# Linear attention and an MLP on one core: chunk one's state from products of 128 rows, alternating output columns, half loads without the zero lanes, and four loads under way

## The chip, the cores and the metric

The kernel runs on one core of a Trainium2 chip as one launch. The metric is the device time of a launch in microseconds (us); the kernel before took 490.62 us, the median of three runs (490.49 to 491.47).

## What is computed

```python
for t in range(S):                                   # S = 768, r, k, v: (4, 8, 768, 48) fp32
    cur = np.einsum('bhd,bhe->bhde', u[None] * kt, vt)
    y[:, :, t] = np.einsum('bhd,bhde->bhe', rt, state + cur)
    state = w[None, :, :, None] * state + np.einsum('bhd,bhe->bhde', kt, vt)
x = y.transpose(0, 2, 1, 3).reshape(3072, 384)
h = x @ w_in                                         # 384 -> 2048
out = (0.5 * h * (1 + erf(h / sqrt(2)))) @ w_out     # 2048 -> 384
```

w and u have one value for each head and channel. All of it is fp32.

## The kernel before, in words

**Attention.** The 768 positions are cut into 6 chunks of 128 positions, in halves h of 64. The 8 heads are taken as 4 pairs, in the order `PAIRS` = 3, 0, 1, 2. A group (`gi`, 0 to 23) is one pair in one chunk, for all 4 batches; groups 0 to 3 are chunk one, and I call them g0 to g3. A group loads two tiles: T (in_rkT) holds r and k transposed, head 0 of the pair on lanes 0 to 47 and head 1 on lanes 64 to 111, with zeros on lanes 48 to 63 that are read along; N (in_rkv) holds k and v by rows of positions.

The steps of a group of chunk one (`first_group`) are these. `prepare` multiplies T by a table E of powers of w (DVE, L426), N's k by the decay WN (POOL, L433), and makes KB = k * u * w (ACT, L444). `scores` (PE, L465) forms k.r into the banks A, `own` the same with KB, `gains` (PE, L476) the sum of k v over 64 positions for each half, which the states are made from, and two `select`s (DVE, L551) put the scores into Am. `gaps` (PE, L515) spreads pair 3's result x3 into the unused lanes of Y for the other three pairs; `old` (PE, L484) adds state times r, `new` (PE, L502) Am times v. `keep` takes Y out of PSUM: an ACT cast into the high part (L565) and a DVE subtraction for the low part (L566). The state after half one is an ACT copy (L532, Sb), the state after half two a DVE multiply and add on two lane quarters (L521, Sa). WN is made from a table of powers by four transposes (PE, L354) and an ACT copy (L357). The table itself is built on DVE: five doublings (L327, 112x8 up to 112x8x15), the power w^32, its reciprocal (L339) and three multiplications of 256 elements.

**MLP.** The weights come in 16 loads of 768 KB into three buffers (raw). Each is split into a high part wh and a low part wl: on ACT wb (L382), wa (L379), the second pass wb (L385) and wh (L391), on DVE wa (L387, L389) and wl (L393). For each chunk there are 16 MLP steps j, 96 in all: nine matmuls of 512 columns for the first layer (L649; high by high, then wl, then the low x), the gelu on ACT (L679), the high and low part of its result on DVE (L680, L681), and nine matmuls of the second layer (L692). During chunk one's 16 steps the PE also does the groups of chunk two, and each step needs a weight that has just been split.

**What sets the order.** A planner written into the kernel (class `Plan`) gives each step a cost and a due time and writes the engines' instruction streams in that order. Where it sees PE idle it puts in "heats" (L311), matmuls on zeros that nobody reads. The loads follow a list, `LOADS` (t0, t1, n0, t2, n1, ...); by `in_turn` a load is issued when the load two places ahead of it in the queue has landed (the first three go at once). T0 and T1 are loaded with 112 lanes, `BARE` = 2; from T2 on a load is two halves of 48 lanes, and the zero lanes are set once by a memset (POOL, L294).

Of the kernel before, what the change touches and what calls it, by code (L numbers as in the profile page):

```python
# [150 lines left out]
def rwkv_gelu_mlp(tc, rkT, rkv, wuT, uN, wmlp, r, k, vT, w, u, out):  # L151
    nc = tc.nc
    with ExitStack() as ctx:
# [31 lines left out]
        E = sb([LP, 2, NP, 2, HALF], F32, "E")  # L185
        P32 = sb([LP, 2, 2 * NP], F32, "P32")
# [139 lines left out]

        def powers():
            nc.vector.memset(one(E0, MID), 1.0)  # L330
            nc.vector.tensor_scalar(out=one(E0, MID + 1), in0=w_sb.unsqueeze(2), scalar1=WMIN, scalar2=WMAX,
                                    op0=ALU.max, op1=ALU.min)
            n = 1
            while n < MID:
                m = min(n, MID - 1 - n)
                times_one(E0[:, :, MID + n + 1:MID + n + 1 + m], E0[:, :, MID + 1:MID + 1 + m], one(E0, MID + n))
                n *= 2
            times_one(P32[:, 0].unsqueeze(2), one(E0, MID + 16), one(E0, MID + 16))
# [609 lines left out]
```

## Time and profile before

| what | us |
|---|---|
| median of three runs | 490.62 |
| the profiled execution | 491.24 |
| its span in the profile | 489.4 |
| PE busy in the span | 477.2 |
| DVE busy | 275.0 |
| ACT busy | 175.8 |
| POOL busy | 67.1 |

The profiled execution took 1.84 us more than its span, for what lies around it, and 0.62 us more than the median. The granted clock was 0.996 of full speed as a mean over the span. PE means TensorE's matmuls, PEld the loading of their stationary operand, which goes beside them. A row of the timeline has the start, the duration, the engine, the line, the operation, the tile written from the tiles read, the count, and in brackets how long the engine had been idle and what ended that.

### The profile page before, as it was taken

Reading aid. Unit: us, or ns where it says so; the run is one execution under the profiler, and the core shown is the slowest. Engines: PE = TensorE matmul, PEld = TensorE weight load, DVE = VectorE, ACT = ScalarE, POOL = GpSimd, SP = SyncE. Lnnn points to the kernel's source line nnn. Section 1 sums busy time; section 2 is a strip of 40 time slices with the busy share of each in tenths; the row PEclk is TensorE's granted clock in tenths of the full one; section 3 lists DMA queues with packets and bytes.
Section 4 is the critical chain, followed back from the end, with each engine's and each line's share of the span. In section 5 each row is a group of like instructions: output and inputs, shape, how many; then the busy total and the mean of one; then the engine's idle time right before and its main releaser. Section 6 shows DMA issues by size and latency. Waiting matters only on the chain.

```text
span 489.4 us, 11700 instructions
## 1 busy us (share of the span) xinstructions
PE 477.2 (98%) x5096; PEld 387.2 (79%) x5096; DVE 275.0 (56%) x446; ACT 175.8 (36%) x353; POOL 67.1 (14%) x85
## 2 busy tenths in 40 slices
PE   7899999999999999999999999999999999999995
PEld 5777787888888887788888878888888887888884
DVE  7689989896646556526536646544654522322221
ACT  6487989843133133131332321331331311211111
POOL 4202101102302022202022022021121100000000
PEclk9999999999999999999999999999999999999998
DMA  6867686513212313303203403123403000100002
GB/s 173 251 205 228 201 252 197 165 37 121 83 34 61 92 37 89 115 10 84 61 33 92 147 1 92 38 57 92 131 17 92 1 11 12 67 1 1 0 0 70
DMA packets 13192, 42.24 MB, mean 86 GB/s; under 512 B 2160, under 2 KB 2544, under 8 KB 13136
## 3 DMA queue, kind: packets, MB, share of 16 engines
q1 hardware_dynamic: 13136, 41.43, 28.9%
q8 instruction: 42, 0.69, 0.6%
q14 instruction: 14, 0.11, 0.1%
HBM read 34.74 MB, written 4.72 MB: 81 GB/s over the span
## 4 chain that ended last, share of the span: by engine, by line
PE 93%; DVE 4%; DMA 1%; issue 1%; SPq 0%; DVEq 0%
PE Hp L649 41%; PE O L692 40%; PE A L465 3%; PE Y L484 3%; PE Y L502 2%; PE Y L476 1%; PE AE L311 1%; PE Y L692 1%; DMA T<-in_rkT_dram 1%; DVE wa L389 1%; DVE Am L551 1%; DVE T L426 0%; PE A L311 0%; DVE wl L393 0%; PE Y L515 0%
## 5 line engine op out<-in xcount | busy, mean ns | idle before, releaser
L649 PE MATMUL Hp<-xx,wh 128*128 128x512 f32 x576 | 166.5, 396 | 0.6 <-ACT wh L391 0.4
L680 DVE CAST gh<-gf 128x512 fp32r<-128x512 f32 x95 | 47.4, 499 | 167.8 <-ACT gf L679 166.8
L679 ACT ACTIVATE gf<-Hp 128x512 f32<-128x512 f32 x96 | 57.4, 597 | 232.9 <-PE Hp L649 219.6
L649 PEld LDWEIGHTS Hp<-xx,wh 128*128 128x128 f32 x576 | 106.9, 188 | 25.9 <-ACT wh L391 1.1
L649 PE MATMUL Hp<-xx,wl 128*128 128x512 f32 x288 | 83.5, 397 | 1.3 <-DVE wl L393 1.1
L692 PE MATMUL O<-gh,wh 128*128 128x512 f32 (+1 forms) x285 | 82.3, 396 | 0.0
L692 PE MATMUL O<-gl,wh 128*128 128x512 f32 (+1 forms) x285 | 80.6, 390 | 0.0
L692 PE MATMUL O<-gh,wl 128*128 128x512 f32 (+1 forms) x285 | 80.6, 390 | 0.0
L681 DVE TENSOR_TENSOR gl<-gf,gh 128x512 fp32r<-128x512 f32 x95 | 74.1, 780 | 10.3 <-DVE gh L680 0.5
L649 PEld LDWEIGHTS Hp<-xx,wl 128*128 128x128 f32 x288 | 53.8, 188 | 15.1 <-DVE wl L393 2.4
L692 PEld LDWEIGHTS O<-gh,wh 128*128 128x128 f32 x285 | 52.2, 188 | 12.5 <-issue 0.3
L692 PEld LDWEIGHTS O<-gl,wh 128*128 128x128 f32 x285 | 52.6, 188 | 11.7
L692 PEld LDWEIGHTS O<-gh,wl 128*128 128x128 f32 x285 | 52.5, 188 | 11.6
L456 ACT ACTIVATE Am<-diag,cs 128x64 f32<-128x64 f32 x120 | 31.7, 338 | 30.4 <-DVE cs L451 30.4
L430 POOL TENSOR_TENSOR Nb<-Nb 128x384 f32<-128x384 f32 x15 | 15.6, 1037 | 125.5 <-DMA Nb<-in_rkv_dram 110.5
L433 POOL TENSOR_TENSOR Nb<-Nb,WN 128x384 f32<-128x384 f32 x20 | 23.5, 1175 | 52.1 <-DMA Nb<-in_rkv_dram 23.0
L426 DVE TENSOR_TENSOR Tb<-Tb,E 112x1024 f32<-112x1024 f32 x20 | 25.2, 1258 | 2.8 <-DMA Tb<-in_rkT_dram 2.7
L521 DVE SCALAR_TENSOR_TENSOR Sb<-Sa,E,Y 48x192 f32<-48x192 f32 x40 | 16.5, 413 | 10.8 <-ACT xx L565 7.0
L493 POOL MEMSET turn<- 1x1 f32 x19 | 1.7, 89 | 130.1 <-PE Y L484 130.1
L448 POOL TENSOR_TENSOR Nb<-Nb,u_sb 128x384 f32<-128x384 f32 x15 | 18.6, 1239 | 0.1
L551 DVE COPY_PREDICATED Am<-past,A 128x512 f32<-128x512 uint32 x24 | 17.7, 738 | 0.4
L565 ACT CAST xx<-Y 112x512 fp32r<-112x512 f32 (+1 forms) x18 | 10.6, 587 | 20.3 <-PE Y L476 14.3
(107 smaller groups left out, 402.0 us busy)
## 6 DMA issues: line engine op xcount, KB each, us to landing
raw<-in_wmlp_dram SPq DMA_DIRECT2D x16, 768.0 KB, 5.2
Nb<-in_rkv_dram SPq DMA_DIRECT2D x15, 576.0 KB, 4.0
Tb<-in_rkT_dram SPq DMA_DIRECT2D x40, 192.0 KB, 3.5
out_dram<-raw SPq DMA_DIRECT2D x5, 768.0 KB, 3.7
Nb<-in_rkv_dram SPq DMA_DIRECT2D x5, 384.0 KB, 3.8
xx<-x SPq DMA_DIRECT2D x30, 64.0 KB, 2.3
N<-in_rkv_dram SPq DMA_DIRECT2D x4, 384.0 KB, 4.0
T<-in_rkT_dram SPq DMA_DIRECT2D x2, 448.0 KB, 4.9
```

The lines of the kernel that those rows point to most:

```text
L426: add("dve", sdve(1024), LATER if g.gi else -10 ** 5, lambda: nc.vector.tensor_tensor(out=flat, in0=flat, in1=E[:, 0, g.p].rearrange("l h ...
L430: add("pool", pool(DM), LATER, lambda: nc.gpsimd.tensor_tensor(out=g.n[:, 0], in0=g.n[:, 0], in1=g.n[:, 1], op=ALU.mult), r=[g.K], w=[g.R])
L433: it = nc.gpsimd.tensor_tensor(out=g.kn, in0=g.kn, in1=WN[:, g.p].rearrange("s j d -> s (j d)").unsqueeze(1).to_broadcast([C, NB, 2 * D]), ...
L448: add("pool", pool(DM), LATER, lambda: nc.gpsimd.tensor_tensor(out=g.n[:, 0], in0=g.n[:, 0], in1=u_sb[:, g.p, :].unsqueeze(1).to_broadcast ...
L456: add("act", sact(HALF) + 60, LATER, lambda x=x, b=b: nc.scalar.activation(out=g.am[:, x, b, :], in_=diag2, func=AF.Copy, scale=g.sums[:, ...
L521: return nc.vector.scalar_tensor_tensor(out=g.s[h + 1][quarter(1 - x)], in0=g.s[h][l], scalar=E[l, 1, g.p, h, MID:MID + 1], in1=gained(g, ...
L551: add("dve", 722, LATER, lambda: nc.vector.copy_predicated(out=g.am, mask=mask.bitcast(U32).unsqueeze(1).unsqueeze(1).to_broadcast([C, 2, ...
L649: nc.tensor.matmul(O[3], lhsT=wt[j][:, 0, k_ * 128:(k_ + 1) * 128], rhs=x[:, a, k_, :], start=start and k_ == ks[0], stop=stop and k_ == k ...
L679: add("act", 600, LATER, lambda: nc.scalar.activation(out=gf, in_=O[3], func=AF.Gelu), r=["H"], w=["gf"])
L680: add("dve", sdve2(512), LATER, lambda: nc.vector.tensor_copy(out=high, in_=gf), r=["gf"], w=[GH])
L681: add("dve", sdve(512), LATER, lambda: nc.vector.tensor_tensor(out=low, in0=gf, in1=high.bitcast(F32), op=ALU.subtract), r=["gf", GH], w=[GL])
L692: nc.tensor.matmul(bank(dst)[:, a:b], lhsT=wt[j][:, 1, d * 128:(d + 1) * 128], rhs=gt[:, a:b], start=(j == 0 and n == 0), stop=(j == NJ - ...
```

## The change

All line numbers of the kernel after are larger by 5 to 48: scores L497, gains L506, old L527, new L545, gaps L558, state L569, L575 and L579, select L598, keep L612 and L613, T's preparation L458, WN's transposes L385, the split L410 to L424, MLP L696, L726 to L728 and L739, heats L316.

1. Loads from the 14th on wait for the load four places ahead, not two (`AHEAD`, `LATE`).
2. T0 and T1 are loaded as halves of 48 lanes like the others, the upper half first; their zero lanes are set by memsets, T0's by DVE as its first instruction, T1's on POOL. Groups 22 and 23 load whole tiles (`WHOLE`).
3. The table of powers is built in another way: powers 0 to 31 (`W`) by the same five doublings, then w^32, w^64, w^96 (`PW`), reciprocals into `ends`, and each pair's table by four products of 64 elements. E[p] of pair 3 comes first, the others when they are needed.
4. In chunk one the second half's gains are 16 matmul passes over all 128 rows; the state after half two is one ACT copy (L575), where two DVE operations were (L521). For later chunks the decay of the second half lies in the tables, and the second state is a plain addition.
5. Each group of chunk one writes Y into the columns of the other half of the bank than the group before (`Y00` to `Y11`), and no longer has to wait until the group before is read out. `old` has a drain of PE ahead of it for g1 to g3.
6. The host no longer swaps the heads of the second half in in_rkv; scores, gains and new index accordingly.

```diff
-            back = UNDERWAY + (len(landing) < START)
+            n = len(landing)
+            back = AHEAD if n >= LATE else UNDERWAY + (n < START)
...
-            if gi < BARE:
+            if gi < WHOLE:
+                in_turn(lambda: [nc.sync.dma_start(T[s][l], rkT[gi][l]) for l in (slice(64, 64 + D), slice(0, D))],
+                        2 * D * 4096, at, [f"T{s}"], first, 2)
+            else:
                 in_turn(lambda: nc.sync.dma_start(T[s], rkT[gi]), LP * 4096, at, [f"T{s}"], first)
...
-        for i in range(BARE, NP):
-            add("pool", 1100, 10 + i, lambda i=i: nc.gpsimd.memset(flat2(T[i])[32:64], 0.0), w=[f"T{i}"])
+        add("dve", 620, -2 * 10 ** 6, lambda: nc.vector.memset(flat2(T[0])[32:64], 0.0), w=["T0"])
+        for i in range(1, NP):
+            add("pool", 1100, 10 + i if i > 1 else -10 ** 6, lambda i=i: nc.gpsimd.memset(flat2(T[i])[32:64], 0.0), w=[f"T{i}"])
...
+        def table(p):
+            out = E[:, p].rearrange("l (a h) (f i) -> l a h f i", h=2, f=2)
+            for a in range(2):
+                for h in range(2):
+                    nc.vector.tensor_tensor(
+                        out=out[:, a, h], in0=W[:, p, h].unsqueeze(1).to_broadcast([LP, 2, MID]),
+                        in1=ends[:, p, 2 + 2 * a + h].unsqueeze(2).to_broadcast([LP, 2, MID]), op=ALU.mult)
...
+                if gi < NP:
+                    g.y, g.Y = YU[:, :, i * U0:i * U0 + U0], [f"Y{x}{i}" for x in range(2)]
...
+            if g.c == 0:
+                for b, x in both:
+                    one(b, x, 0, times(0), x)
+                for b, x in both:
+                    one(b, x, 1, slice(0, C), x)
...
         def old(g):
+            if 0 < g.gi < NP:
+                nc.tensor.drain()
...
+            if g.c == 0 and h:
+                add("act", 330, at, lambda: nc.scalar.copy(out=g.s[2], in_=gained(g, 1, slice(0, LP))), r=[g.U[1]], w=g.S[2])
+                return
```

The order of the loads changes with it. On SP, which issues them, the program begins before with the following rows (T_102 is g0's T, N_110 its N; 112x1024 is lanes by elements).

```order
L268 DMA wu_sb<-in_wuT_dram 112x16
L251 DMA T_102<-in_rkT_dram 112x1024
L251 DMA T_103<-in_rkT_dram 112x1024
L260 DMA N_110<-in_rkv_dram 128x768
L253 DMA T_104<-in_rkT_dram 48x1024 [waits DMAHW2_49,Pool_49]
```

And now (T_105 is g0's T, N_113 its N):

```order
L272 DMA wu_sb<-in_wuT_dram 112x16
L264 DMA N_113<-in_rkv_dram 128x768
L255 DMA T_105<-in_rkT_dram 48x1024
L255 DMA T_105<-in_rkT_dram 48x1024 [waits DVE_49]
L255 DMA T_106<-in_rkT_dram 48x1024
```

N of g0 now stands ahead of T of g0, whose second half waits for the memset on DVE.

On PE, the end of chunk one and the start of the MLP read before (A, Y and UE are PSUM banks, AE is written by heats, Hp is the first layer's bank, T_105 and N_113 are g3's tiles):

```order
L476 MATMUL UE<-N_113 48x48 [waits DMAHW3_49,DVE_49,Pool_49]
L476 MATMUL UE<-N_113 48x48 x15
L311 MATMUL AE<-zeros 128x256 x13
L515 MATMUL Y<-x_122,spread 128x256 [waits DVE_49]
L515 MATMUL Y<-x_122,spread 128x256 x3
L484 MATMUL Y<-T_105,Sb 48x64 [waits Activation_49] x2
L484 MATMUL Y<-T_105,Sb 48x64 x6
L502 MATMUL Y<-Am_117,N_113 48x64 x16
L311 MATMUL AE<-zeros 128x256
```

And now, with T_107 and N_115 for g2, T_108 and N_116 for g3:

```order
L316 MATMUL AE<-zeros 128x256 x4
L506 MATMUL UE<-N_116 48x48 [waits DMAHW4_49,Activation_49]
L506 MATMUL UE<-N_116 48x48 x15
L527 MATMUL Y<-T_107,Sb 48x64 x8
L545 MATMUL Y<-Am_119,N_115 48x64 x16
L527 MATMUL Y<-T_108,Sb 48x64 [waits Activation_49] x2
L527 MATMUL Y<-T_108,Sb 48x64 x6
L545 MATMUL Y<-Am_120,N_116 48x64 [waits DVE_49]
L545 MATMUL Y<-Am_120,N_116 48x64 x15
L696 MATMUL Hp<-xx_123,wh_75 128x512 [waits PE_49]
```

The products of g2 and g3 stand behind each other, where a wait for DVE and 13 heats stood between; in chunk one 25 heats are gone.

On ACT, the casts of g2 and g3 and the split of the second weight (raw_129) stand before as follows:

```order
L565 CAST xx_120<-Y 128x2x4x64 [waits DVE_49,PE_49]
L532 COPY Sb<-UE 48x192 [waits DVE_49,PE_49]
L532 COPY Sb<-UE 48x192
L391 CAST wh_75<-wa_131 128x768 [waits DVE_49]
L382 ACTIVATE wb_135<-raw_129 128x768 [waits DMAHW4_49]
L379 ACTIVATE wa_132<-raw_129 128x768
L565 CAST xx_120<-Y 128x2x4x64 [waits DVE_49,PE_49]
L385 ACTIVATE wb_135<-raw_129 128x768 [waits Activation_49]
```

And now (the second weight is raw_132; KB_111 is of chunk two):

```order
L612 CAST xx_123<-Y 128x2x4x64 [waits DVE_49,PE_49]
L476 ACTIVATE KB_111<-Tb_109,uw 112x4x64 [waits DMAHW7_49,DMAHW6_49,DVE_49]
L612 CAST xx_123<-Y 128x2x4x64 [waits DVE_49]
L413 ACTIVATE wb_138<-raw_132 128x768 [waits DMAHW0_49]
L410 ACTIVATE wa_135<-raw_132 128x768
L416 ACTIVATE wb_138<-raw_132 128x768 [waits Activation_49]
L726 ACTIVATE gf<-Hp 128x512 [waits PE_49]
L476 ACTIVATE KB_111<-Tb_109,uw 112x4x64
L476 ACTIVATE KB_112<-Tb_110,uw 112x4x64 [waits DMAHW3_49,DMAHW2_49,DVE_49]
L476 ACTIVATE KB_112<-Tb_110,uw 112x4x64
L422 CAST wh_76<-wa_135 128x768 [waits DVE_49]
```

Two passes of the second weight's split stood ahead of g3's cast; all three now stand behind both casts. The first of those casts, g2's, waits for the end of g3's `new` on PE.

## Rows read from the trace of the kernel before

**Rows 1.** The page: busy time of each engine; instruction fetch (transfers, MB, share).
```profile
PE 477.2 (98%) x5096; PEld 387.2 (79%) x5096; DVE 275.0 (56%) x446; ACT 175.8 (36%) x353; POOL 67.1 (14%) x85
...
q8 instruction: 42, 0.69, 0.6%
```

**Rows 2.** Windows: stretch, length, busy of PE, PEld, DVE, ACT, POOL, clock, DMA, GB/s.
```profile
60.00:70.00 10.00, 10.00 (x194) 8.22 (x193) 9.19 (x13) 7.93 (x13) 0.81 (x2) 1.00 0.84 293
```

**Rows 3.** The chain that ended last, its first transfer: start, duration, what.
```profile
1.29 4.34 DMA T<-in_rkT_dram
```

**Rows 4.** Timeline, DVE and SP at the start.
```profile
2.65 1.28 DVE L327 TENSOR_TENSOR E<-E 112x8 f32<-112x8 f32 x5
...
4.05 0.20 DVE L339 RECIPROCAL P<-P 112x8 f32<-112x8 f32 x1
...
5.73 1.23 DVE L426 TENSOR_TENSOR T<-T,E 112x1024 f32<-112x1024 f32 x1 [1.01 <-DMA T<-in_rkT_dram]
6.87 0.17 DVE L348 TENSOR_TENSOR uw<-wu_sb,E 112x8 f32<-112x8 f32 x1
...
7.33 0.79 SPq L253 DMA_DIRECT2D T<-in_rkT_dram  x2
```

**Rows 5.** Timeline, from the transposes for WN to the first gains.
```profile
7.98 0.57 PE L354 MATMUL AE<-ident,E 112*128 112x112 f32 x4
...
10.22 0.45 PEld L476 LDWEIGHTS UE<-N 64*48 64x48 f32 x32 [0.58 <-POOL N L433]
```

**Rows 6.** Timeline, PEld: halts that end with "issue".
```profile
14.23 0.18 PEld L502 LDWEIGHTS Y<-Am,N 64*48 64x48 f32 x8 [0.89 <-issue]
...
19.18 0.49 PEld L465 LDWEIGHTS A<-T 48*64 48x64 f32 x27 [0.15 <-issue]
...
23.59 0.36 PEld L476 LDWEIGHTS UE<-N 64*48 64x48 f32 x22 [0.52 <-issue]
```

**Rows 7.** Timeline, PE at the end of chunk one.
```profile
27.19 1.82 PE L311 MATMUL AE<-zeros 128*128 128x256 f32 x13
...
30.15 0.67 PE L502 MATMUL Y<-Am,N 64*48 64x64 f32 x32
```

**Rows 8.** Timeline, ACT and one row of DVE around the start of the MLP.
```profile
29.68 0.90 ACT L379 ACTIVATE wa<-raw 128x768 f32<-128x768 f32 x1
30.88 0.59 ACT L565 CAST xx<-Y 128x512 fp32r<-128x512 f32 x1 [0.30 <-PE Y L502]
31.36 1.09 ACT L385 ACTIVATE wb<-raw 128x768 f16<-128x768 f32 x1
...
31.63 0.69 DVE L566 TENSOR_TENSOR xx<-Y,xx 128x512 fp32r<-128x512 f32 x1
...
32.31 0.89 ACT L444 ACTIVATE KB<-Tb,uw 112x256 f32<-112x256 f32 x2
33.88 0.60 ACT L679 ACTIVATE gf<-Hp 128x512 f32<-128x512 f32 x1 [0.68 <-PE Hp L649]
34.37 0.83 ACT L391 CAST wh<-wa 128x768 fp32r<-128x768 f32 x1
...
39.17 0.84 ACT L391 CAST wh<-wa 128x768 fp32r<-128x768 f32 x1 [0.65 <-DVE wa L389]
```

**Rows 9.** Timeline, PEld: first-layer loads of weights that waited for a split.
```profile
35.25 0.53 PEld L649 LDWEIGHTS Hp<-xx,wh 128*128 128x128 f32 x3 [0.24 <-ACT wh L391]
...
43.18 0.53 PEld L649 LDWEIGHTS Hp<-xx,wl 128*128 128x128 f32 x3 [1.56 <-DVE wl L393]
...
49.92 0.53 PEld L649 LDWEIGHTS Hp<-xx,wh 128*128 128x128 f32 x3 [0.89 <-ACT wh L391]
...
51.03 0.52 PEld L649 LDWEIGHTS Hp<-xx,wl 128*128 128x128 f32 x3 [0.58 <-DVE wl L393]
```

**Rows 10.** Waits of SP's queue and of ACT, 0 to 60 us: us in total, times, longest.
```profile
SPq L364 <- ACT wb L385: 1.7, 1, 1.7
...
ACT xx L565 <- PE Y L502: 3.4, 3, 2.1
```

More of the change, by code (lines that the diff above doesn't have):

```diff
@@ new lines, in powers @@
+            w16 = W[:, :, :, 16]
+            mult(PW[:, 0], w16, w16)
+            mult(PW[:, 1], PW[:, 0], PW[:, 0])
+            mult(PW[:, 2], PW[:, 0], PW[:, 1])
+            nc.vector.tensor_copy(out=ends[:, :, 5], in_=PW[:, 0:2, :, 1].rearrange("l f p -> l p f"))
+            nc.vector.reciprocal(out=ends[:, :, 3, 0], in_=PW[:, 2, :, 1])
+            nc.vector.reciprocal(out=ends[:, :, 3, 1], in_=PW[:, 1, :, 1])
+            for a in (2, 4):
+                nc.vector.reciprocal(out=ends[:, :, a, 0], in_=PW[:, 0, :, 0])
@@ new lines, in powers @@
+            table(PAIRS[0])
+        def state_powers():
+            mult = lambda out, x, y: nc.vector.tensor_tensor(out=out, in0=x, in1=y, op=ALU.mult)
+            mult(PW[:, 3], PW[:, 1], PW[:, 1])
+            for s in range(2):
+                nc.vector.tensor_copy(out=ends[:, :, s], in_=PW[:, 2 - 2 * s:4 - 2 * s, :, 0].rearrange("l f p -> l p f"))
+                mult(ES[:, :, s].rearrange("l p (f i) -> l p f i", f=2),
+                     W[:, :, 0].unsqueeze(2).to_broadcast([LP, NP, 2, MID]),
+                     ends[:, :, s].unsqueeze(3).to_broadcast([LP, NP, 2, MID]))
@@ L352, in flip @@
+        add("dve", 3000, 5, powers, r=["w_sb"], w=["E0", "Ep3"])
+        add("dve", 1000, LATER, state_powers, r=["E0"], w=["E1"])
+        add("dve", 160, LATER, lambda: nc.vector.tensor_tensor(out=uw, in0=u_lane, in1=W[:, :, :, 1].rearrange(
+            "l p h -> l (p h)"), op=ALU.mult), r=["w_sb", "E0"], w=["uw"])
+        for p in PAIRS[1:]:
+            add("dve", 530, LATER, lambda p=p: table(p), r=["E0"], w=[f"Ep{p}"])
         def flip():
             for p in range(NP):
-                nc.tensor.transpose(AE[:, 1, p * 128:p * 128 + LP], E[:, 1, p].rearrange("l h i -> l (h i)"), ident[:LP, :LP])
+                nc.tensor.transpose(AE[:, 1, p * 128:p * 128 + LP], ES[:, p].rearrange("l h i -> l (h i)"), ident[:LP, :LP])
@@ L472, in gains, with one @@
         def gains(g):
-            for b in range(NB):
-                for x in range(2):
+            def one(b, x, h, t, j):
+                nc.tensor.matmul(g.u[quarter(x), h, g.u0 + b * D:g.u0 + (b + 1) * D], lhsT=g.kn[t, b, heads(j)],
+                                 rhs=g.vn[t, b, heads(j)], start=True, stop=True)
+            both = [(b, x) for b in range(NB) for x in range(2)]
+            if g.c == 0:
[3 more added lines that the diff above has]
+                    one(b, x, 1, slice(0, C), x)
+            else:
+                for b, x in both:
                     for h in range(2 if g.more else 1):
-                        nc.tensor.matmul(g.u[quarter(x), h, g.u0 + b * D:g.u0 + (b + 1) * D], lhsT=g.kn[times(h), b, heads(x)],
-                                         rhs=g.vn[times(h), b, heads(x)], start=True, stop=True)
+                        one(b, x, h, times(h), x ^ h)
         def old(g):
+            if 0 < g.gi < NP:
+                nc.tensor.drain()
             for b in range(NB):
@@ L586, in first_group @@
             if spreads(g):
-                add("pe", 460, LATER, lambda: gaps(g), r=["spread", "x3h", "x3l"], w=g.Y)
-            add("pe", 1150, LATER, lambda: (old(g), new(g)), r=[g.T, g.V, g.AM] + g.S[1], w=g.Y)
+                add("pe", 650, LATER, lambda: gaps(g), r=["spread", "x3h", "x3l"], w=g.Y)
+            add("pe", 1300, LATER, lambda: (old(g), new(g)), r=[g.T, g.V, g.AM] + g.S[1], w=g.Y)
             keep(g, LATER)
```

78 lines of the change are left out of this document (35 added, 43 removed).

## The prediction

> **What bounds the kernel now.** I read the page first. PE is busy 477.2 of 489.4 us [rows 1], so only the 12.2 us in which it is idle, or work that it does for nothing, can be won. The windows tell where that lies: from 60 to 70 us PE is busy 10.00 of 10.00 [rows 2], and the last wait of PE for anything is the one that ends at 51.03 [rows 9]. After that point the MLP runs matmul behind matmul and the change leaves its 18 passes a step alone. What counts is therefore how much earlier or later PE stands at the same step after 51 us.
>
> The chain of waits begins with the first transfer of T, 1.29 to 5.63 us [rows 3], goes on over T's preparation on DVE, which had waited 1.01 us for that transfer [rows 4], to the transposes at 7.98 and the first gains at 10.22 [rows 5]. From there PE carries the chain to the end of g3's `new`, 30.15 + 0.67 = 30.82 [rows 7]. ACT casts that result from 30.88, finishes the second weight's split and writes its wh at 34.37 [rows 8]; step j = 1 waits for that until 35.25. Later steps wait again for a weight, until 43.18, 49.92 and 51.03 [rows 9].
>
> Three halts inside chunk one end with "issue", at 14.23, 19.18 and 23.59 [rows 6]: PE waits for no other engine there. Counted along PE, they stand 130 and 129 matmuls apart. With the weight load that goes with each this is some 260 instructions, and the page's 42 instruction transfers for two times 5096 are 243 each [rows 1]. I read these halts as PE arriving at the end of what has been fetched. The spacing in time, from the first gains on, is 4.01, 4.95 and 4.41 us, a mean of 4.46.
>
> **The first transfer.** T0 was 112 lanes of 4096 bytes, 458,752, with nothing but the small wu_sb ahead of it. Now N of g0 (393,216 bytes) stands ahead of T0's two halves (393,216), so 786,432 bytes must pass until T0 is there, 327,680 more. T1 landed when SP issued the next load, 7.33, after T0's 5.63 [rows 3, 4]: 458,752 bytes in 1.70 us, 270 bytes a ns. So T0 lands 1.2 us later, at 6.84. If nothing queued, it would be -0.24 (65,536 bytes less); I take the full 1.2, since T1's landing shows that a queue is what the second load meets. The memset on DVE lies ahead of the arrival of wu_sb and costs nothing; if it came late it would hold only the lower half of T0.
>
> DVE's table must be ready too. The five doublings end at 3.93 [rows 4]. Then come 17 small operations: three products, a copy, four reciprocals, eight products of 64 elements, uw. Where one needs the result of the one before, the step is 0.20 to 0.26 (the reciprocal; 1.28 over five); where not, the next starts 0.09 before the end (uw at 6.87 against 6.96), about 0.15. Seven of the first kind and ten of the second are 3.0 us: 6.9. The bounds are 6.5 and 8.3 (all of one kind). So preparation of T0 starts at **6.9**, with data and table together.
>
> **To the first gains.** Before it took 2.25 us from preparation to the transposes. The state's table now needs a product and two copies besides its two halves of 256 elements, and uw has gone ahead: +0.3 (bounds 0 and 0.6). From the transposes to the gains it was 2.24 [rows 5], with no new step in it. That gives 6.9 + 2.55 + 2.24 = **11.7**, 1.5 us later than before.
>
> **Through chunk one.** From the first gains to the end of g3's `new` stand 568 matmuls before and 544 now: 25 heats are gone. In both the fourth fetch boundary is the last to cross; it now lies about 20 matmuls ahead of the end. At 4.46 us each the four are crossed at 11.7 + 17.8 = 29.5; 20 of 32 matmuls of `new` are 0.4 [rows 7], and the gains over 128 rows, which take both row halves of the array and cannot go two at a time, together with a drain add 0.4 (0.3 to 0.8 by the half rate, one of four groups on the path). So g3's `new` ends at **R = 30.3**, 0.5 earlier than now. The heats removed were worth 1.82 us before g3 alone [rows 7], and the wait of `gaps` for DVE that alternating columns remove lay under them; if fetch sets the pace, neither is won.
>
> A page of the Trainium skill speaks against this: "Runtime: NRT & Kernel Launch", section "Instruction fetch mechanics", says that blocks of 256 instructions are fetched while the one before is executed and that crossing a boundary is mostly hidden. The trace agrees on the size of the block and not on the hiding (0.89, 0.15 and 0.52 us of halt); by the page R would come out as in the second rival.
>
> **ACT's order.** Before, two passes of the second weight (wb, wa) went ahead of g3's cast. Now g2's cast itself waits for the end of g3's `new`, and all three passes stand behind both casts. From R: cast 0.59, DVE's low part 0.69, cast 0.59, wb 0.8, wa 0.9, wb again 0.95 (1.09 less its overlap), gelu 0.5, three KB 1.3, wh 0.83 [rows 8], which is 7.15; with 0.25 for the handing over, 7.4. Step j = 1 starts at R + 7.4 = **37.7**, 2.45 later than 35.25 [rows 9].
>
> That alternate columns of a bank don't let g2's cast go beside g3's product is what the Trainium skill says too ("PSUM — Partial Sum Buffer", section "PSUM bank collisions raise a hardware error": bank and partition quadrant count, not the address). With g2's cast and low part free to go earlier, the sum would be 0.59 + 0.69 = 1.3 us less.
>
> **What is taken back.** Ahead of the wh for j = 2 ACT sat idle 0.65 us at 39.17 [rows 8]; that absorbs as much, so j = 2 waits until 43.18 + 1.8 = 45.0. The two later waits (0.89 and 0.58 [rows 9]) shrink when PE arrives later, as far as ACT and DVE are not late themselves: bounds 0 and 1.4; I take 0.4, since the wait for wh and the one for wl follow the same late split. The sum in terms of R is R - 27.85 - 0.65 - 0.4 = **R - 28.9**, and for R = 30.3 it is +1.4.
>
> **Edits that I cost at nothing.** The four loads under way: only one wait of SP's queue for a buffer and none of ACT or PE for a raw weight is among the large ones before 60 us [rows 10], and afterwards PE waits for nothing. If that cover were gone, it would be a landing later by a load, 768 KB at 270 bytes a ns, 2.9 us, ahead of one split. The plain addition of the second state and the heads that are no longer swapped leave the counts of later chunks as they are. The state copy on ACT takes two DVE operations off, in a stretch where DVE is not last. POOL's memset of T1 is its first work and ends before SP needs it.
>
> The profiled execution took 491.24; +1.4 makes 492.6. It lay 0.6 above the median, so against the median I say **492.0**. No change means within 0.2%, 1.0 us, which is what a measurement here can tell.
>
> **Rivals.** *No change, 490.2.* The pace of the first interval, 4.0 us, holds for all four: R = 11.7 + 16 + 0.8 = 28.5, the sum is -0.4. One interval of three is that short, and the other two are not; a larger share of the later waits absorbed gives the same. From R = 27.9 to 29.9 it stays within the bound. 0.30.
>
> *Faster, 488.7.* Boundaries cost nothing as such, and the halts were PE arriving early. Then the engines set R. DVE has the last word: for each group a preparation 1.23 and two selects of some 0.73, with tables and low parts, bring it to about 23.5 from 8.5; then gains, `old` and `new` of g2 and g3 follow, so R lies between 25 and 30, and the middle is 27. The sum is R - 28.9 = -1.9. For it speaks that the halt at 19.18 is only 0.15 long, and that the heats before it were idle time; against it that three of three boundaries halt. It decides below R = 27.9. 0.20.
>
> *Heavier, 494.0.* The pace is 4.95 (loads in flight where instructions are fetched), or the table takes the whole 8.3: R = 32.3, the sum is +3.4. 0.08.
>
> My forecast itself, R from 29.9 to 31.5, has 0.42: slower by 1.0 to 2.6 us.
>
> **How the numbers follow.** Slower is 0.42 + 0.08 = 0.50, no change 0.30, faster 0.20. The range goes from 488.8, which leaves half of the faster case out, to 494.2, which takes in most of the heavier one.
>
> **What would show it.** Preparation of T0 at 6.9 with the load of T0 as releaser; first gains at 11.7; halts with "issue" near 16.2, 20.6, 25.1 and 29.5; the casts of g2 and g3 both behind R = 30.3; j = 1 waiting for wh until 37.7; the j = 2 wait until about 45.0; later waits shorter than 0.9. It would be wrong if chunk one ends near 27 with no halts, if j = 1 starts before 35.25, or if PE waits for a weight again behind 55 us.

## The result

The changed kernel takes 497.9 us (median of four runs, 496.55 to 507.15), the kernel before 490.56. The ratio is 1.0138, with a 95% interval of 1.0120 to 1.0156: 1.4% slower. The forecast had the sign and the wrong size: 492.0, range 488.8 to 494.2. The times of the changed kernel lie further apart than those of the kernel before. In some runs of these kernels the mean granted clock is lower and the time longer (here 507.15 us at 0.971), and the ratios leave those out: one of the changed kernel's four, one each of e2, e9, e10, e15 and e16, two of e13's five and two of e4's four.

The profiled execution took 496.73 us, its span is 495.0, 5.6 more than before. The page of the changed kernel, against [rows 1]:

```profile
PE 479.2 (97%) x5074; PEld 387.2 (78%) x5074; DVE 272.5 (55%) x464; ACT 177.2 (36%) x357; POOL 67.3 (14%) x86
...
q8 instruction: 41, 0.67, 0.6%
```

PE has 22 matmuls less and is busy 2 us longer. Where it is idle the windows show (columns as in [rows 2]):

```profile
20.00:25.00 5.00, 4.83 (x129) 4.00 (x127) 4.85 (x7) 3.45 (x6) 2.93 (x2) 1.00 0.81 224
25.00:30.00 5.00, 4.10 (x89) 3.43 (x90) 3.39 (x5) 1.70 (x6) 0.05 (x1) 1.00 0.86 251
...
40.00:50.00 10.00, 8.33 (x110) 5.82 (x114) 8.81 (x15) 9.20 (x12) 1.11 (x2) 1.00 0.54 186
50.00:60.00 10.00, 10.00 (x130) 8.27 (x123) 9.14 (x15) 8.70 (x13) 0.00 (x0) 1.00 0.96 294
...
100.00:150.00 50.00, 48.45 (x596) 39.32 (x595) 30.86 (x52) 17.39 (x38) 7.80 (x10) 1.00 0.23 65
```

The last line is the surprise: this one loses 1.55 us between 100 and 150. The kernel before loses nothing there:

```profile
100.00:150.00 50.00, 50.00 (x604) 40.57 (x603) 33.80 (x60) 15.77 (x36) 7.23 (x9) 1.00 0.27 74
```

The start, from the chain of waits (first row) and the timeline of the changed kernel, against [rows 3 to 5]:

```profile
2.22 5.03 DMA T<-in_rkT_dram
...
7.38 1.23 DVE L458 TENSOR_TENSOR T<-T,E 112x1024 f32<-112x1024 f32 x1 [0.26 <-DMA T<-in_rkT_dram]
...
10.03 0.57 PE L385 MATMUL AE<-ident,ES 112*128 112x112 f32 x4 [0.25 <-DVE ES L367]
...
12.66 0.93 PEld L506 LDWEIGHTS UE<-N 64*48 64x48 f32 x32 [0.97 <-POOL N L465]
```

T0 lands at 7.25, the first gains start at 12.66. PE's halts (idle times that end with "issue") and the end of chunk one, against [rows 6, 7]; in these rows PEld has the halts some 0.15 us longer than PE:

```profile
16.61 0.22 PEld L545 LDWEIGHTS Y<-Am,N 64*48 64x48 f32 x9 [0.56 <-issue]
...
26.46 0.66 PEld L506 LDWEIGHTS UE<-N 64*48 64x48 f32 x19 [0.91 <-issue]
...
31.86 0.91 PE L545 MATMUL Y<-Am,N 64*48 64x64 f32 x32
...
89.83 0.57 PE L506 MATMUL Y<-Nb 64*48 64x48 f32 x30 [0.26 <-issue]
...
109.19 0.47 PE L506 MATMUL Y<-Nb 64*48 64x48 f32 x25
111.21 0.30 PE L506 MATMUL Y<-Nb 64*48 64x48 f32 x7 [1.55 <-issue]
```

g3's product ends at 32.77. ACT behind it, against [rows 8], and the waits of the first layer's weight loads, against [rows 9]:

```profile
32.82 0.59 ACT L612 CAST xx<-Y 128x512 fp32r<-128x512 f32 x1 [2.29 <-PE Y L545]
...
34.17 0.59 ACT L612 CAST xx<-Y 128x512 fp32r<-128x512 f32 x1 [0.35 <-DVE xx L613]
34.65 0.91 ACT L413 ACTIVATE wb<-raw 128x768 uint32<-128x768 uint32 x1
35.45 0.89 ACT L410 ACTIVATE wa<-raw 128x768 f32<-128x768 f32 x1
...
38.97 0.83 ACT L422 CAST wh<-wa 128x768 fp32r<-128x768 f32 x1
```

```profile
39.85 0.53 PEld L696 LDWEIGHTS Hp<-xx,wh 128*128 128x128 f32 x3 [0.41 <-ACT wh L422]
41.48 0.53 PEld L696 LDWEIGHTS Hp<-xx,wl 128*128 128x128 f32 x3 [1.10 <-DVE wl L424]
...
46.14 0.53 PEld L696 LDWEIGHTS Hp<-xx,wh 128*128 128x128 f32 x3 [1.34 <-ACT wh L422]
47.20 0.53 PEld L696 LDWEIGHTS Hp<-xx,wl 128*128 128x128 f32 x3 [0.53 <-DVE wl L424]
```

ACT sat idle 2.29 us ahead of g2's cast, with the second weight's passes queued behind it.

So of the 5.6 us some 2.9 are there at MLP step 4 (57.54 against 54.63). The rest comes after it: from step 8 to step 15 the changed kernel takes 36.78 us and the kernel before 34.55. Those are the numbers that the experiments go by. "Chunk one" is the end of g3's product; a step is the start of its first matmul of the first layer; all are read from the timeline of the profiled execution.

| kernel | chunk one | step 1 | step 4 | steps 8 to 15 | ratio to before (95%) |
|---|---|---|---|---|---|
| before | 30.81 | 35.27 | 54.63 | 34.55 | |
| changed | 32.77 | 39.86 | 57.54 | 36.78 | 1.0138 (1.0120 to 1.0156) |
| e1 boundaries moved | 39.74 | 47.07 | 65.03 | 34.46 | 1.0136 (1.0097 to 1.0175) |
| e2 two loads | 33.37 | 40.05 | 57.02 | 38.90 | 1.0120 (1.0074 to 1.0167) |
| e3 before, fewer heats | 30.34 | 34.86 | 54.04 | 39.14 | 1.0047 (1.0020 to 1.0073) |
| e4 order on ACT | 35.16 | 43.16 | 58.38 | 35.03 | unclear |
| e5 T0 whole | 32.31 | 38.98 | 57.33 | 34.48 | 1.0041 (1.0024 to 1.0057) |
| e6 64 rows | 32.47 | 37.44 | 54.89 | 35.71 | 1.0057 (1.0037 to 1.0077) |
| e7 more heats | 33.34 | 41.20 | 58.85 | 34.46 | 1.0126 (1.0053 to 1.0198) |
| e8 before, four loads | 31.50 | 35.98 | 54.77 | 35.51 | 1.0026 (1.0009 to 1.0043) |
| e9 e5 + e6 | 31.61 | 36.03 | 57.56 | 34.43 | 1.0048 (1.0032 to 1.0064) |
| e10 e9, two loads | 31.66 | 36.06 | 53.55 | 34.98 | 1.0036 (1.0015 to 1.0057) |
| e11 e10, order on ACT | 32.80 | 37.86 | 54.74 | 34.79 | 1.0026 (1.0006 to 1.0046) |
| e12 e9, Y not alternating | 33.07 | 36.29 | 55.13 | 34.45 | 1.0020 (0.9999 to 1.0041) |
| e13 order on ACT, few heats | 33.28 | 39.03 | 54.62 | 36.06 | 1.0044 (1.0024 to 1.0065) |
| e14 before, Y alternating | 30.39 | 35.44 | 55.33 | 35.09 | 1.0085 (1.0056 to 1.0115) |
| e15 e12, two loads | 38.75 | 41.95 | 59.19 | 34.99 | 1.0026 (1.0010 to 1.0043) |
| e16 e13 + heats, boundaries moved | 33.20 | 39.70 | 55.29 | 34.47 | 1.0059 (1.0037 to 1.0080) |

Some entries hold a stretch in which the clock was granted below 1.00, so they aren't the edit's cost alone: chunk one in e1 and e15 (below) and in e3, steps 8 to 15 in e2 and e3, and step 4 in e9. The windows of e2, of e3 (three) and of e9:

```profile
110.00:115.00 5.00, 3.61 (x12) 2.87 (x13) 2.65 (x5) 1.82 (x3) 0.00 (x0) 0.73 0.10 22
...
15.00:20.00 5.00, 5.00 (x134) 4.47 (x138) 3.86 (x7) 3.20 (x7) 0.09 (x1) 0.66 0.84 275
...
85.00:90.00 5.00, 2.97 (x120) 2.63 (x111) 3.41 (x6) 2.53 (x4) 0.07 (x1) 0.82 0.78 264
90.00:95.00 5.00, 5.00 (x20) 3.97 (x19) 4.14 (x6) 3.38 (x5) 0.00 (x0) 0.84 0.48 82
...
50.00:55.00 5.00, 3.43 (x9) 2.45 (x10) 4.97 (x7) 3.90 (x5) 0.00 (x0) 0.72 0.89 244
```

### The profile page after: what moved, and what is told of

It reads as the page before. It is cut to its first block, busy times and chain, and to the rows that moved or that the text cites. A ratio compares the mean times of both kernels' runs of the same rounds, so it can differ in the third digit from the quotient of the medians.

```text
span 495.0 us, 11682 instructions
## 1 busy us (share of the span) xinstructions
PE 479.2 (97%) x5074; PEld 387.2 (78%) x5074; DVE 272.5 (55%) x464; ACT 177.2 (36%) x357; POOL 67.3 (14%) x86
## 4 chain that ended last, share of the span: by engine, by line
PE 93%; DVE 3%; issue 1%; DMA 1%; ACT 1%; POOL 0%; SPq 0%; DVEq 0%
PE O L739 40%; PE Hp L696 40%; PE Y L527 3%; PE A L497 3%; PE Y L545 3%; PE Y L506 1%; PE Y L739 1%; DMA T<-in_rkT_dram 1%; PE UE L506 1%; PE AE L316 1%; DVE wa L420 0%; DVE wl L424 0%; PE Y L558 0%; POOL N L465 0%; DVE gl L728 0%
## 5 line engine op out<-in xcount | busy, mean ns | idle before, releaser
L696 PE MATMUL Hp<-xx,wh 128*128 128x512 f32 x576 | 166.8, 397 | 1.2 <-ACT wh L422 1.2
L726 ACT ACTIVATE gf<-Hp 128x512 f32<-128x512 f32 x96 | 57.4, 598 | 231.3 <-PE Hp L696 225.8
L727 DVE CAST gh<-gf 128x512 fp32r<-128x512 f32 x95 | 46.0, 484 | 168.2 <-ACT gf L726 168.0
L696 PEld LDWEIGHTS Hp<-xx,wh 128*128 128x128 f32 x576 | 106.9, 188 | 27.6 <-ACT wh L422 1.8
L696 PE MATMUL Hp<-xx,wl 128*128 128x512 f32 x288 | 83.3, 396 | 0.8 <-DVE wl L424 0.7
L739 PE MATMUL O<-gh,wh 128*128 128x512 f32 (+1 forms) x285 | 82.3, 396 | 0.0
L739 PE MATMUL O<-gh,wl 128*128 128x512 f32 (+1 forms) x285 | 80.7, 390 | 0.0
L739 PE MATMUL O<-gl,wh 128*128 128x512 f32 (+1 forms) x285 | 80.5, 389 | 0.0
L728 DVE TENSOR_TENSOR gl<-gf,gh 128x512 fp32r<-128x512 f32 x95 | 73.5, 774 | 9.5
L696 PEld LDWEIGHTS Hp<-xx,wl 128*128 128x128 f32 x288 | 54.0, 188 | 14.3 <-DVE wl L424 1.6
L739 PEld LDWEIGHTS O<-gh,wh 128*128 128x128 f32 x285 | 52.1, 188 | 12.4 <-issue 0.3
L739 PEld LDWEIGHTS O<-gl,wh 128*128 128x128 f32 x285 | 52.6, 188 | 11.6
L739 PEld LDWEIGHTS O<-gh,wl 128*128 128x128 f32 x285 | 52.5, 188 | 11.6
L465 POOL TENSOR_TENSOR Nb<-Nb,WN 128x384 f32<-128x384 f32 x20 | 22.3, 1114 | 58.1 <-DMA Nb<-in_rkv_dram 29.8
L458 DVE TENSOR_TENSOR Tb<-Tb,E 112x1024 f32<-112x1024 f32 x20 | 24.4, 1218 | 3.2 <-DMA Tb<-in_rkT_dram 3.0
L569 DVE SCALAR_TENSOR_TENSOR Sb<-Sa,PW,Y 48x192 f32<-48x192 f32 x40 | 16.5, 413 | 10.1 <-ACT xx L612 6.8
L612 ACT CAST xx<-Y 112x512 fp32r<-112x512 f32 (+1 forms) x18 | 10.6, 587 | 23.0 <-PE Y L506 18.9
L613 DVE TENSOR_TENSOR xx<-Y,xx 112x512 fp32r<-112x512 f32 (+1 forms) x18 | 12.4, 689 | 10.1 <-ACT xx L612 9.8
```

The costliest lines, as they stand in the source:

```text
L458: add("dve", sdve(1024), LATER if g.gi else -10 ** 5, lambda: nc.vector.tensor_tensor(out=g.t, in0=g.t, in1=E[:, g.p].rearrange("l (a h) i ...
L465: it = nc.gpsimd.tensor_tensor(out=g.kn, in0=g.kn, in1=WN[:, g.p].rearrange("s j d -> s (j d)").unsqueeze(1).to_broadcast([C, NB, 2 * D]), ...
L569: return nc.vector.scalar_tensor_tensor(out=out, in0=s_, scalar=PW[quarter(x), 3, g.p, 0:1], in1=more, op0=ALU.mult, op1=ALU.add)
L696: nc.tensor.matmul(O[3], lhsT=wt[j][:, 0, k_ * 128:(k_ + 1) * 128], rhs=x[:, a, k_, :], start=start and k_ == ks[0], stop=stop and k_ == k ...
L726: add("act", 600, LATER, lambda: nc.scalar.activation(out=gf, in_=O[3], func=AF.Gelu), r=["H"], w=["gf"])
L727: add("dve", sdve2(512), LATER, lambda: nc.vector.tensor_copy(out=high, in_=gf), r=["gf"], w=[GH])
```

## The experiments

**The late halts.** Three kernels ask whether they come from where the instruction blocks end. A block is what one transfer of q8 brings (0.67 MB in 41 transfers on the page); its end is a boundary.

```diff
 e1, changed kernel
-                        plan, "heat", None if plan.over else (lambda: heat(A[0]), 234, SHARE))] + [
+                        plan, "heat", None if plan.over else (lambda: short(A[0]), 234, SHARE))] + [
+        def short(dst):
+            heat(dst[:, 0:256], 256)
+            for _ in range(4):
+                nc.tensor.matmul(dst[0:16, 0:16], lhsT=zeros[:, 0:16], rhs=zeros[:, 0:16], start=True, stop=True)
 e2, changed kernel
-UNDERWAY, START, AHEAD, LATE = 2, 3, 4, 13
+UNDERWAY, START, AHEAD, LATE = 2, 3, 2, 13
 e3, kernel before
-LEEWAY, SHARE = 700, 0.9
+LEEWAY, SHARE = 700, 0.45
```

> Edit: the heats between MLP steps 0 and 1 of the changed kernel become one of 256 columns and four of 16x16 each, so that some 40 more matmuls stand ahead of chunk two's products; nothing else. Theory A (instruction blocks): the 0.26 and 1.55 us of halt at 89.8 and 111.2 come from a block boundary near the start of a burst of 160 short matmuls, with the next boundary 127 later in the same burst; moved by 40, the boundaries lie elsewhere, no halt over 0.3 us after 51 us, span 495.0 - 2 = 493.0 (492.3 to 493.7). Rival B (loads in flight slow the fetch, or run-to-run scatter): the halts stay in the groups of chunk two, span 494.6 to 496.

> Edit: loads from the 14th on wait for the one two places ahead again; PE's stream stays word for word. Theory A: the halts at 89.8 and 111.2 stay within 0.5 us, and the span stays within 0.8 us of 495.0. Rival B (four loads under way slow the fetch): the 1.55 us halt goes and the span is 493 to 493.7. Rival C (the four loads bring weights forward): steps 1 to 4 are later, span over 496.

> Edit: kernel before, the share of idle time that heats may fill 0.45 instead of 0.9, which takes some 30 matmuls out of chunk one and the start of the MLP; nothing else. Theory A: chunk two's bursts now meet the boundaries as the changed kernel does, a halt with issue of 0.5 to 1.6 us appears near 105 us, and the kernel gets slower by 0.5 to 2 us although it does less; the halts inside chunk one get longer where heats are gone. Rival D (heats are idle time that costs nothing, and what ends chunk one is other engines): same time within 0.3 us, or faster where a heat was in the way. If the granted clock falls below 1.0 in a window, neither is tested.

e1 has no halt in the bursts any more: steps 8 to 15 take 34.46 us, about as before the change (34.55). From step 4 to the end of the span it takes 435.1 us, the changed kernel 437.5 and the kernel before 434.8. e2 keeps its halt, near the same place (matmul 1622 instead of 1621), 1.83 us long; the loads do not make it. Its stream on PE is that of the changed kernel up to matmul 771 and not, as its text has it, to the end. Its span, 497.2, is longer than Theory A said, with the lower clock behind that halt. And e3 gives the kernel before a halt that it never had, by leaving out 30 matmuls that compute nothing (timeline of e3, PE):

```profile
88.40 0.72 PE L476 MATMUL Y<-Nb 64*48 64x48 f32 x22 [2.03 <-issue]
```

The halt is the one that Theory A foretold. e3 is also slower, by 0.47%, but its text on record leaves the two undecided where the clock falls, and in this trace it fell twice, behind the halt at 88.40 and behind one of 1.28 us at 14.95. What the halt costs by itself isn't shown.

Counted along PE in the traces, the halts stand at matmul 221, then some 127 further or a multiple of it (474, 1366, 1621), in kernels whose work at these places differs. In chunk two a burst of `old`, `scores`, `own`, `new` and `gains` is 160 short matmuls. Up to step 15, where a boundary falls 11 to 34 matmuls into a burst, the next one falls at its end or close behind, some 2 us later, and PE halted for 0.36 to 2.03 us: in the changed kernel, e2, e3 (twice), e4, e6 and e13, all that have such a place. The other kernels show no halt over 0.3 us in these bursts, with one exception (e8, 0.53). Behind a burst, under a long matmul, e12 has one of 1.70 us until 52.92, and e15, with the same count, has none there.

Two boundaries in one burst are not enough. The kernel before has them too, 4 and 131 matmuls into its burst at 103.96, and does not halt. What differs is when the second block is fetched. In the changed kernel no instruction transfer starts between 104.3 and 107.3, where its burst begins; one starts behind that, ahead of the resumption at 111.21 (first line: the DMA queues of the changed kernel from 108 to 111). In the kernel before it starts ahead of the burst (second line: from 101 to 103.9).

```profile
q8 instruction: 1, 0.02, 2.1%
...
q8 instruction: 1, 0.02, 2.3%
```

By the start times of these transfers in the traces, PE went on 2.3 to 3.2 us after the start in each of the halts above. Where the transfer started 0.4 us or more ahead of a burst with two boundaries, there was no halt.

The Trainium skill ("Runtime: NRT & Kernel Launch", section "Instruction fetch mechanics") has blocks of 256 instructions and calls the crossing mostly hidden. The count agrees with the size: 127 matmuls with their weight loads are 254. Under long matmuls most crossings are hidden in the traces (e12's 1.70 us and 0.55 us in e3 are not); in bursts of short ones they cost up to 2.03 us.

e1's time was no shorter all the same. One reason is in the windows of the profiled execution, the longest of its four:

```profile
15.00:20.00 5.00, 3.13 (x84) 2.66 (x78) 2.90 (x6) 2.29 (x6) 0.00 (x0) 0.89 0.61 150
20.00:25.00 5.00, 4.83 (x95) 4.02 (x97) 2.75 (x4) 3.56 (x6) 2.57 (x2) 0.50 0.67 177
25.00:30.00 5.00, 5.00 (x79) 4.29 (x79) 2.02 (x3) 1.39 (x3) 0.00 (x0) 0.50 0.98 289
30.00:35.00 5.00, 5.00 (x74) 4.48 (x75) 3.44 (x4) 0.95 (x3) 1.00 (x1) 0.50 0.95 315
```

The halt at matmul 221 lasted 1.78 us in this execution (0.41 in the changed kernel's profile), and behind it the clock was granted at 0.50, the lower level of 1.2 GHz, for 15 us; chunk one ended 7 us late. The same halt of 1.78 us in e2, and one of 1.75 in e13, was followed by no such fall. What decides it wasn't found. Such falls can be why times of these kernels differ by more than those of the kernel before. e1's shortest two, 496.71 and 497.12 us, are no better than the changed kernel's either, so the 2.4 us that its profile has gained behind step 4 are not seen in its times.

**The order on ACT.**

```diff
 e4, changed kernel
+        w_split(1)
         for gi in range(NP):
             first_group(gi)
-                w_split(G)
+                G == 1 or w_split(G)
-            add("act", 590, at, lambda: nc.scalar.copy(out=view(dst[l, 0]), in_=src), r=g.Y, w=[f"{XN}h"])
+            add("act", 590, at, lambda: nc.scalar.copy(out=view(dst[l, 0]), in_=src), r=g.Y + (["wa1", "wb1s"] if g.gi == 2 else []), w=[f"{XN}h"])
 e13, on top of e4
-                        plan, "heat", None if plan.over else (lambda: heat(A[0]), 234, SHARE))] + [
+                        plan, "heat", None if plan.over else (lambda: heat(A[0]), 234, 0.4))] + [
```

> Edit: changed kernel, the three ACT passes of the second weight stand ahead of g2's cast (a dependency for the planner alone). ACT sat idle 2.29 us ahead of that cast. Theory E (the order on ACT cost j = 1 some 2.7 us): j = 1 starts near 37.0 instead of 39.85, and after the later waits 1 to 2.5 us are left of that: span 492.5 to 494. Rival F (the later steps are bound by the splits that follow, whatever j = 1 does): j = 1 earlier, yet span within 0.6 us of 495.0.

> Edit: changed kernel, the second weight's three ACT passes ahead of g2's cast as in e4, and the heats between MLP steps 0 and 1 at a share of 0.4, so that they don't stand where the weight is ready; T0, gains, columns and loads as changed. Theory E (of the 4.6 us that j = 1 is late, some 2.5 are the order on ACT): j = 1 within 5 us of the end of g3's product (7.1 in the changed kernel, 5.0 in e6 where the planner came to another order), and 1 to 2 us earlier at step 4. Rival F: the distance stays near 7 because another engine is last. The late halt of 1 to 1.8 us stays (the boundary lies 28 into the last burst).

e4 tells little: the planner, which thought PE idle there, put 19 heats (4.47 us) into step 0, two halts of 1.60 and 1.37 us fell into chunk one, and its times gave no ratio. e13 answers the question. T0 in halves, 128 rows, columns, tables and loads are all as changed (beside the order, 8 heats around step 0 instead of 10), chunk one ends even 0.5 us later, at 33.28, and yet step 4 is at 54.62, where the kernel before has it. ACT no longer idles ahead of the cast (timeline of e13):

```profile
30.81 0.89 ACT L413 ACTIVATE wb<-raw 128x768 uint32<-128x768 uint32 x1
31.59 0.89 ACT L410 ACTIVATE wa<-raw 128x768 f32<-128x768 f32 x1
32.37 1.08 ACT L416 ACTIVATE wb<-raw 128x768 f16<-128x768 f32 x1
33.34 0.59 ACT L612 CAST xx<-Y 128x512 fp32r<-128x512 f32 x1
```

The text on record missed in two points: step 1 stands 5.75 us behind chunk one's end, not within 5, and gained only 0.8; and step 4 gained 2.9, not 1 to 2, since the rest was won at steps 2 to 4, whose weights follow on ACT. The ratio fell from 1.0138 to 1.0044. The late halt stayed, 1.27 us.

**The parts undone one at a time.**

```diff
 e5, changed kernel
-            if gi < WHOLE:
+            if 0 < gi < WHOLE:
-        add("dve", 620, -2 * 10 ** 6, lambda: nc.vector.memset(flat2(T[0])[32:64], 0.0), w=["T0"])
 e6, changed kernel: gains and state of chunk one as in later chunks
-            if g.c == 0:
-                for b, x in both:
-                    one(b, x, 0, times(0), x)
-                for b, x in both:
-                    one(b, x, 1, slice(0, C), x)
-            else:
...
-            if g.c == 0 and h:
-                add("act", 330, at, lambda: nc.scalar.copy(out=g.s[2], in_=gained(g, 1, slice(0, LP))), r=[g.U[1]], w=g.S[2])
-                return
...
-                if g.c == 0:
+                if g.c == 0 and h == 0:
 e7, changed kernel
-LEEWAY, SHARE = 700, 0.9
+LEEWAY, SHARE = 700, 1.4
 e8, kernel before
-            back = UNDERWAY + (len(landing) < START)
+            back = 4 if len(landing) >= 13 else UNDERWAY + (len(landing) < START)
 e14, kernel before: Y00 to Y11 and the drain in old, as in the change
```

> Edit: changed kernel, T0 loaded whole as before (112 lanes, ahead of N0), no memset on DVE for it. Theory G (the late start goes through to the end): T0 lands near 5.6, its preparation starts at 6.4 where the table binds, first gains near 11.6 instead of 12.66, and the span is 1.0 shorter, 494.0, halts aside. Rival H (halts at block boundaries and the order on ACT eat it): first gains earlier, but j = 1 and the span within 0.5 us of the changed kernel's.

> Edit: changed kernel, chunk one's second gains over 64 rows and its second state from two DVE additions, as in later chunks. Theory I: gains take 0.58 us a group again instead of 1.06, and chunk one ends 0.5 to 1 us earlier (g3's product ends by 32). Rival J: the DVE additions come back on the path and give that up; end of chunk one within 0.3 us of 32.7.

> Edit: changed kernel, the heats' share of idle time 1.4 instead of 0.9: some 18 matmuls on zeros more, 66 up to the third MLP step where the kernel before has 70; nothing else. Theory A: long matmuls ahead of a block boundary give the next block time to come, so the halts of chunk one shrink (the 0.78 us at 25.7 most), the clock does not fall, and the runs spread less; the span is no longer, 494 to 495.2, though 18 matmuls are added. Rival D (heats delay what stands behind them): longer by 1 us or more, 496 and up.

> Edit: kernel before, and of the change only the four loads under way from the 14th on. Theory A and the prediction (loads are not waited for): same time, within 0.2% of the kernel before. Rival C (weights come forward and steps 2 to 4 wait less): faster by 0.5 to 1.5 us, the waits at 43.18 to 51.03 shorter. Rival B (more loads beside instruction fetch): slower by over 1 us with longer halts.

> Edit: kernel before, and of the change only the alternating columns of Y with the drain. Theory N (they take the read out off chunk one's path, e12 ended chunk one 1.5 us later without them): g3's product ends 0.5 to 1.5 us ahead of 30.8. Theory M: it ends as before, since gains, halts and selects set it. Time: within 0.2% of the kernel before either way, as steps 1 to 3 are bound by the splits.

e5: the first gains come at 11.62, 1.04 earlier, as written, and by step 4 only 0.2 of that is left (57.33). Its span, 492.9, is shorter than either theory said, for another reason: its stream has 17 matmuls more, the boundaries lie elsewhere, and steps 8 to 15 take 34.48. e6: the end of chunk one moves by 0.3 only, so Theory I falls; but the planner came to another order on ACT, with two passes of the second weight ahead of g3's cast, and step 4 is at 54.89. Both are the two places above, reached by the way. e7 lost its halts (0.41 us until 16.46 is the only one left in chunk one) and paid at step 1, 41.20, since the added heats stood where PE was wanted: Theory A right on the halts, wrong on the time.

e8: with four loads under way the kernel before is slower by 0.26%. Step 4 is 0.1 later in its profile, behind a wait of 1.16 us for that step's weight, and a halt of 0.53 us stands at 107.04, in a stream with two matmuls more. So Rival B's longer halts are there too, and which of the two costs the 0.26% stays open. In e9 against e10 step 4 is at 57.56 against 53.55, because a wait of 1.88 us for the weight of step 3 appears and the clock falls behind it (0.72 from 50 to 55 us). e2, the changed kernel with two loads, is no faster than the changed kernel.

e14: the columns alone end chunk one 0.42 us earlier and cost 0.85%, where within 0.2% had been expected; the wait for the weight of step 2 is longer (1.54 us against 1.12), and step 4 is 0.7 later. Why, was not followed up; of the two parts of the change that were tried on the kernel before alone it is the larger loss.

**Together.** e9 is e5 and e6, e10 to e12 and e15 take more of the change away (edits as above; e11 has e13's order on ACT, e12 and e15 have each group's Y in the same columns again), e16 is e13 with the share 1.4 and e1's `short` with three small matmuls.

> Edit: changed kernel with both undone, T0 loaded whole and the gains and state of chunk one as in later chunks (e5 and e6 together); the tables, the alternating columns and the four loads stay. Theory K (the two losses are separate places on the path, the late start and the gains with the ACT order behind them): first gains near 11.5, g3's product ends near 31, no halt over 0.3 us after 51 us (the block boundaries lie 50 and more matmuls into the bursts), ratio to the kernel before 0.998 to 1.002. Rival L (both gave back the same us, the late halt and the heats): ratio 1.004 or more, as each alone.

> Edit: e9 and loads from the 14th on two places ahead again. After e8 (four under way made the kernel before 0.26% slower): 1 us faster than e9, ratio 0.996 to 1.000, steps 2 to 4 as early or earlier. Rival (the loads matter only together with other bounds): the same as e9 within 0.2%.

> Edit: e10, and the second weight's ACT passes ahead of g2's cast, as in e4, with the heats between MLP steps 0 and 1 cut (share 0.4), which in e4 stood 19 deep where the weight was ready. Theory E (the order on ACT): j = 1 within 4.5 us of the end of g3's product, where the changed kernel needed 7.1, and 0.5 to 1 us faster than e10. Rival F: j = 1 earlier, the time as e10.

> Edit: e9 without the alternating columns of Y (each group of chunk one waits again until the one before is read out). Theory M (alternating columns are worth little, since cast and product follow each other anyway): within 0.2% of e9. Rival N (they take the read out off the path): e9 is 1 us or more faster than this.

> Edit: changed kernel without T0 in halves, 128 rows, alternating columns and four loads: what stays is the way the tables are built, the plain addition of the second state in later chunks and the heads not swapped. Theory (each of the four was a loss or nothing): 1 us faster than e12, ratio 0.997 to 1.001. Rival (the tables on DVE, ready at 6.3 where T0 lands at 5.6, hold the start by 1 us to the end): ratio 1.002 and up.

> Edit: e13 (the order on ACT), with the heats of chunk one at a share of 1.4 as in e7, and those between MLP steps 0 and 1 as one of 256 columns and three of 16x16 each, which moves the block boundaries out of the last bursts; T0 in halves behind N0, 128 rows, tables, columns and four loads all as changed. If the two causes (the order on ACT, and halts at block boundaries) make up the loss, it is back at the kernel before though chunk one still starts 2 us late: no halt over 0.3 us after 51 us, step 4 near 54.6, ratio 0.999 to 1.003. If the late start, the gains or the loads cost something by themselves: ratio 1.004 and more.

e9 is no better than e5 alone: the gains do not add, as Rival L had it. What holds its profile back is the wait for the weight of step 3 with the clock's fall behind it. With two loads under way (e10) the wait is gone; the ratios, 1.0048 and 1.0036, don't tell the two apart. The order on ACT wins nothing over e10 (e11: 1.0026, step 4 at 54.74 against 53.55, with a halt of 1.28 us in chunk one). e12 can't be told from the kernel before, and its ratio is below e9's, so Rival N falls there: e9 is not faster. e15's profiled execution had its clock at 0.78 to 0.88 between 15 and 35 us, behind a halt of 1.84, so its steps aren't comparable; its ratio is no better than e12's. e16 keeps every part of the change and mends both places: no halt after 51 us, steps 8 to 15 in 34.47, a span of 490.3 against 495.0 for the changed kernel and 489.4 before. By its profile the loss of 5.6 us is down to 0.9. By its times 0.59% remains of 1.38%, no less than in e13, which kept the late halt. So the second case of its text came, 1.004 or more: the two places make up the loss in the profile, but some of the time goes elsewhere, and which part of the change that is stays open. The columns (e14) are the first candidate.

No version beat the kernel before.

## Why the prediction was wrong

Two steps failed: the pace that gave R, the end of chunk one, and "After that point the MLP runs matmul behind matmul". By the profile, term by term: +1.4 us was said. R came 2.5 later than said, ACT's order took 0.3 less, and 0.6 more was taken back, which makes the 2.9 us at step 4. Behind it come 2.7 us for which the sum had nothing, 2.2 of them from step 8 to 15. Together that is the 5.6.

- **Sign.** Slower by over 0.2% had the largest chance, and the way there began as described. The size was off by a factor of five against the median of the runs shown (7.3 instead of 1.4), by four in the profiled executions (5.5).
- **The first transfer, and to the first gains.** T0 at 6.84 came out at 7.25, its preparation at 6.9 at 7.38, the gains at 11.7 at 12.66. The memset on DVE, costed at nothing, held up the table by 0.8 us (the doublings start at 3.45, not 2.65; at 2.72 in e5, which has no such memset), which the late transfer covered. The first decay on POOL took 1.40 us where it had taken 1.02.
- **Through chunk one, R = 30.3.** This step failed in size. R was 32.77: 1.0 from the start, and 20.1 us from the first gains on where 18.6 was said. Four halts at 4.46 us were to set that time; two are in the trace, 0.41 and 0.78 us, so PE did not wait for instructions at each boundary. (Before, the three halts stand 127 matmuls apart, not 130 and 129.) Gains took 1.06 us for each group where 0.54 to 0.58 had been, and I had added 0.4 for one. But e6, which takes that back, ends chunk one only 0.3 earlier, since PE waits for the casts there (1.3 us). What sets the rest of R stays open.
- **ACT's order.** This step was right, and so was its size: step 1 stands 7.1 us behind R, 7.4 was said. That g2's cast would wait for g3's product while the second weight's split stands behind it is what costs the 2.9 us at step 4 (e13). Whether the cast could go beside the product no run shows.
- **What is taken back, R - 28.9.** 1.05 us was said between step 1 and step 4, 1.7 came; j = 2, foretold until 45.0, waited until 47.20. The form is not borne out either: the sum carries R on to the end one for one. e13 ends chunk one 2.5 us later than the kernel before and has nothing of it left at step 4. In e5 step 1 is 0.9 earlier than in the changed kernel and step 4 only 0.2; in e7 both are 1.3 later. What the weights' order on ACT leaves decides at step 4, more than when chunk one ends.
- **"After that point the MLP runs matmul behind matmul."** This step failed as a term put at nothing. I had read the halts as block boundaries, counted the matmuls, and used the count inside chunk one alone. The 22 matmuls taken out (24 heats fewer in chunk one, not 25, and 2 more behind it) move every later boundary too, and in two of chunk two's bursts the second block then comes too late: 0.26 and 1.55 us of halt, 2.2 us from step 8 to 15. With the boundaries moved the same steps take 34.46 (e1, e7).
- **Edits costed at nothing.** Four loads under way: +0.26% on the kernel before (e8), with another place of the boundaries in it, and no difference in the changed kernel (e2). The columns, from which I expected neither gain nor loss, cost 0.85% on the kernel before (e14).
- **The rivals.** *Faster* rested on heats being idle time. e3 shows that removing 30 of them, and nothing else, gives the kernel before a halt of 2.03 us, and that it is slower. *Heavier* has the R nearest to what came, 32.3, and another mechanism: PE halted at two boundaries and not at four, and the table was ready at 7.0, not 8.3.

## What to carry to other kernels

A matmul that computes nothing still has a place in the instruction stream: when the number of matmuls ahead of a dense burst changes, count where the instruction blocks end in the bursts behind it, down to the end of the program. When an engine works in the order written, look for what stands behind an instruction that waits for the end of a stage; here the split of the next weight, worth 2.9 us at step 4, waited behind a cast and nothing else. And a saving at the start is only worth what is left of it at the first place where another engine is last.

## What was not expected of the hardware

A halt at the same place in the stream lasts differently from one profile to the next: at matmul 221 it took 0.41 us in the changed kernel and 1.78 in e2, whose stream on PE is the same up to there; 0.41 to 1.28 in most others, and 1.75 to 1.84 in e1, e13 and e15. In e1 and e15 such a long halt was followed by 15 to 20 us with the clock granted at 0.50 to 0.88, in e2 and e13 it was not. In e2 the late halt of 1.83 us was, in e3 one of 1.28 and one of 2.03, and in e9 a wait of 1.88 us for a weight; after 1.70 us (e12) and 1.55 (the changed kernel) the clock stayed at 1.00. In e1 PE was busy 4.8 to 5.0 of every 5 us from 20 to 35 us, and still got the lower clock.
